# Attention scores of tiles 2 to 4 as three fp32r products of high and low parts instead of one fp32 product

## The chip, the cores and the metric

The kernel runs on one core of one Trainium2 chip. The metric is the device time of one execution in microseconds (us). Engines are named as the profile names them: PE (TensorE matmul), PEld (its weight loads), DVE (VectorE), ACT (ScalarE), POOL (GpSimd), SP (SyncE).

## The reference, cut to what matters

A block-causal attention over 8 batches of 8 heads (576 positions, head dimension 64, blocks of 64 positions), whose output goes into a mixture of experts with one expert per token.

```python
# q, k, v: (8, 8, 576, 64), all fp32
scores = scale * np.matmul(q, k.transpose(0, 1, 3, 2))      # scale = 1/8
mask = block_i >= block_j                                    # blocks of 64 positions
scores = np.where(mask, scores, -1000000000.0)
attn = np.exp(scores - np.max(scores, axis=-1, keepdims=True))
attn = attn / (np.sum(attn, axis=-1, keepdims=True) + 1e-09)
x = np.matmul(attn, v)                                       # -> (4608, 512)
...
# experts: 8 of them, 512 -> 1024 -> 512; the token's best expert by x @ w_gate
h = np.maximum(xe @ w1[e], 0.0)
out[mask] = gate_w[mask, None] * (h @ w2[e])
```

## The kernel before

The work has two parts in time: the attention, up to about 365 us of the profile, then the experts.

**Units, tiles, turns.** The attention goes through 32 units `m`; a unit is two heads of one batch, one in partitions 0 to 63 and one in 64 to 127 of the tiles `qd` and `kd` (queries and keys, head dimension in partitions). Its 576 query rows are a first block of 64 (tile 0) and four tiles of 128 (tiles 1 to 4). Tile `i` sees `e = 64 + 128 i` keys: 192, 320, 448 and 576. The products of tile `i` are one fp32 matmul per head (two for tile 4, whose 576 columns lie in two halves of 288): queries as weights, 64 rows by 128 columns, keys as the moving operand. PSUM names: tile 4's scores lie in `xa` and `xb` (first and second head), those of tiles 1 to 3 in `ya` and `yb`.

**The order of the work** is written out by hand in the table `ORDER`. One pass over it is a turn; a word such as `S4:2` means step `S4` for the unit `turn - 2`. In each turn every engine gets its instructions in the order of the table, and each engine works through its own strictly in that order. The steps that matter here:

- `ld` (SP): loads `qd`, `kd` and the values of a unit (three buffers each for the first two).
- `pQ` (POOL, L114): `q = 0.125 * qd`, 128x640, two buffers. It must wait for `S0` of the unit two before, the last to read that buffer.
- `S1` to `S4` (PE, L171): the scores. `S0` (PE, L160): those of tile 0, both heads in one matmul.
- `K`, `M` (DVE, L182, L187): mask of a block, row maximum. `E` (ACT, L202): exponential with row sums, written to `pb`.
- `R1`, `R2` (DVE): reciprocal of the sums. `Z` (POOL, L215): scales tile 0's row of probabilities, waits for `R2`.
- `T` (PE, L241): four 128x128 transposes of `pb` into one of two PSUM buffers `pt`. `H` (ACT, one of them on DVE; L253): copies it out to `ph`. `V` (PE, L272): probabilities times values, output `o`. `O`, `F`, `X`, `Y`: output copied, folded with the gate's weights, scaled.
- `y` (POOL): one item of a list, if there is one: a scatter of the router's table (an indirect DMA, L697), or one half of splitting a chunk of the first expert's weights (L1514, L1517). `z`: a piece of the router's work on DVE.

On PE a turn is: `Ta1, S0, S4, Tb1, Tk0, F1, Ta2, Tb2, F2, F0, Tx3, Tt0, S1, S2, S3, V0` to `V4`, `V5`; the next turn's `Ta1` follows. `E1` to `E3` of a unit fall at the end of the turn of its `S1` to `S3`, and the first transposes of the same unit open the next turn.

**fp32 and fp32r.** An fp32 matmul of the program shows as two instructions in the trace, an fp32r one as one. The experts' part already computes in fp32r: an operand `x` is split into a high part, `x` rounded to fp32r, and a low part, `x - high`, and a product is the sum of high*high, high*low and low*high in PSUM.

Of the kernel before, what the change touches and what calls it, by code (L numbers as in the profile page):

```python
# [8 lines left out]
F32 = mybir.dt.float32  # L9
F32R = mybir.dt.float32r  # L10
# [7 lines left out]
P = 128  # L18
H = 8
S = 576  # L20
D = 64
# [17 lines left out]
class Attention:  # L39
# [8 lines left out]
    def __init__(self, ctx, tc, ident, qT, kT, vt, w_gate, ends, po):  # L48
        self.tc, self.nc = tc, tc.nc
        self.qT, self.kT, self.vt = qT, kT, vt  # L50
        self.po = po

        self.ends = ends.rearrange("p (i c) -> p i c", c=P)
        self.M = qT.shape[0] * H // 2
        nc = self.nc
        cp = ctx.enter_context(tc.tile_pool(name="acst", bufs=1))
        self.raw = ctx.enter_context(tc.tile_pool(name="araw", bufs=3))
        self.rawv = ctx.enter_context(tc.tile_pool(name="arawv", bufs=5))
        self.spl = ctx.enter_context(tc.tile_pool(name="aspl", bufs=2))
        self.pt = ctx.enter_context(tc.tile_pool(name="apt", bufs=9))  # L60
        self.sm = ctx.enter_context(tc.tile_pool(name="asm", bufs=3))
        self.ot = ctx.enter_context(tc.tile_pool(name="aot", bufs=2))
        self.xp = ctx.enter_context(tc.tile_pool(name="axp", bufs=2))
        self.ps = ctx.enter_context(tc.tile_pool(name="psa", bufs=1, space=PSUM))
        self.ps_t = ctx.enter_context(tc.tile_pool(name="pst", bufs=2, space=PSUM))

        self.cp, self.ident = cp, ident
        self.raws, self.qs = {}, {}
        self.pb, self.sums, self.neg, self.rs = {}, {}, {}, {}
        self.bank, self.ptile, self.ph, self.oT, self.xs = {}, {}, {}, {}, {}  # L70
        self.small_bank, self.at = (None, None), {}
        self.used, self.later = {}, []
        self.op_ld(0)
        self.op_ld(1)
        self.zero = cp.tile([P, D], F32, tag="zero", name="zero")
        nc.vector.memset(self.zero, 0.0)

        self.h0 = [cp.tile([P, P], F32, tag=f"h0{i}", name=f"h0{i}") for i in range(2)]
        for t in self.h0:
            nc.gpsimd.memset(t, 0.0)  # L80
        self.p0 = {}
        self.o0 = [cp.tile([P, P], F32, tag=f"o0{i}", name=f"o0{i}") for i in range(2)]
        for t in self.o0:
            nc.gpsimd.memset(t, 0.0)
        self.eps = cp.tile([P, 9], F32, tag="eps", name="eps")
        nc.gpsimd.memset(self.eps, 1e-9)

        self.fold = cp.tile([P, H // 2, FC], F32, tag="fold", name="fold")
        nc.vector.memset(self.fold, 0.0)
        nc.scalar.copy(self.fold[:, :, 0:P], ident[:, None, :].to_broadcast([P, H // 2, P]))  # L90
        wg = w_gate.rearrange("(m j d) e -> j d m e", d=D, j=2)
        for j in range(2):
            nc.sync.dma_start(self.fold[D * j : D * j + D, :, P + E * j : P + E * j + E], wg[j])
# [17 lines left out]
    def op_pQ(self, m):  # L111

        q = self.qs[m] = self.spl.tile([P, 512 + P], F32, tag="q", name=f"q{m}")
        self.nc.gpsimd.tensor_scalar(q, self.raws[m][0][:, 0 : 512 + P], 0.125, None, ALU.mult)  # L114

    def banks(self, m, x):

        if (m, x) not in self.bank:
            shape, tag = ([P, 2, 512], "s" + x[1]) if x[0] in "xy" else ([P, 512], x[:2].rstrip("-"))
            self.bank[m, x] = (self.po if x == "o" else self.ps).tile(shape, F32, tag=tag, name=f"{x}{m}")  # L120
        return self.bank[m, x]
# [33 lines left out]
    def op_S(self, m, i):  # L155

        mm = self.nc.tensor.matmul
        q, k = self.qs[m], self.raws[m][1]
        if i == 0:
            mm(self.part(1, m, "S0", 432, 496), q[:, 512:], self.raws[m][0][:, 512 + P :], start=True, stop=True)  # L160
            return
        e = 64 + 128 * i
        for c in range(2 if i == 4 else 1):
            for j in range(2):
                out, _ = self.region(m, i, j)
                if i == 4:
                    out = out[:, c]
                n = out.shape[-1]
                o = (0 if j else S - e) + n * c
                r = slice(64 * j, 64 * j + 64)  # L170
                ins = mm(  # L171
                    out, q[r, 128 * (i - 1) : 128 * i], k[r, o : o + n], start=True, stop=True, skip_group_check=True
                )
                self.uses(m, i, j, ins)

    def op_K(self, m, i, j):

# [153 lines left out]
    def step(self, name, m):  # L331

        name, _, engine = name.partition("@")
        k = name[0]
        if name in ("ld", "pQ", "R1", "R2", "Z"):
            getattr(self, "op_" + name)(m)
        elif name in ("O", "O0"):
            getattr(self, "op_" + name)(m, engine)
        elif k == "H":
            self.op_H(m, name[1:], engine)  # L340
        elif k == "T":
            self.op_T(m, name[1:])
        elif k == "Y":
            self.op_Y(m, int(name[1]), engine)
        elif k in "KME":
            getattr(self, "op_" + k)(m, int(name[1]), int(name[2:] == "B"))
        else:
            getattr(self, "op_" + k)(m, int(name[1]))
# [65 lines left out]


ORDER = """
E3B:3 V5:4 z2:0 O0@D:4 ld:0 Ta1:3 O@A:4 Ha1@A:3 S0:3 S4:2 z6:0 M0:3 Tb1:3 Tk0:3 pQ:1 K4B:2 E0:3 R1:3 K4A:2 z1:0 M4B:2
R2:3 F1:4 Hb1@A:3 Ta2:3 Hk0@A:3 X1:4 Y1:4 M4A:2 Tb2:3 F2:4 E4B:2 y0:0 Z:3 Hb2@D:3 F0:4 Ha2@A:3 Y2:4 z4:0 Tx3:3 Tt0:3
E4A:2 X2:4 S1:2 z5:0 z0:0 z3:0 Ht0@A:3 Y0@D:4 S2:2 K1A:2 K2A:2 S3:2 K1B:2 Hx3@A:3 K2B:2 V0:3 V2:3 M2A:2 K3A:2 M1B:2
M3A:2 E2A:2 E1B:2 V1:3 y1:0 E3A:2 V3:3 M1A:2 K3B:2 M2B:2 E1A:2 M3B:2 V4:3 E2B:2  # L420
"""
# [397 lines left out]
class Experts:  # L819
# [62 lines left out]
    def run(self):  # L882
# [471 lines left out]
        def work(t):  # L1354

            engines = (dve, sp)
            to = ((lambda: blocks(t),), (lambda: move(sp, t),))
            plans = [[step(engine, i) if i > 1 else None for i in (t - 1, t)] for engine in engines]
            for engine, rest, (before, now) in zip(engines, to, plans):
                if t > 2:  # L1360
                    with engine.If(now[4] < 1):
                        for x in rest:
                            x()
                    engine.end_ifs()
                    units(engine, before, 1, split if engine is dve else refill(t - 1))
                units(engine, now, 0, split if engine is dve else refill(t))
                if t > 2:
                    with engine.If(now[4] > 0):
                        for x in rest:
                            x()  # L1370
                    engine.end_ifs()
# [229 lines left out]
```

## Time and profile before

| | |
|---|---|
| median of 3 runs | 809.85 us (809.34 to 810.65) |
| profiled execution | 810.1 us, its span 808.4 us |
| PE, ACT, DVE, POOL busy in the span | 781.2, 400.0, 471.8, 389.7 us |
| scores' matmuls (L171), columns 288: xa and xb, 128 instructions each | 41.6 us busy each |
| 320 and 448: ya and yb, 64 instructions each | 22.9 and 30.0 us busy each |
| pQ (L114), 32 times | 58.0 us busy, 1811 ns one |

A row of the timeline has start, duration, engine, line, operation, output and input by the program's names, the shape, the count, and in brackets the idle time of the engine before it with what ended it. [...] Rows of groups, with a bar, have busy time and mean duration of a group, then the idle time before it.

### The profile page before, as it was taken

What the parts mean: (1) busy time and instruction counts of PE and PEld (TensorE: products, weight loads), DVE (VectorE), ACT (ScalarE), POOL (GpSimd) and SP (SyncE); (2) the same over time, 40 slices, a digit from 0 to 9 for tenths busy, and PEclk for the clock granted to TensorE, in tenths of its full rate; (3) what the DMA queues carried; (4) which work ended last, traced back from release to release, by engine and by line L of the source; (5) the groups of instructions that cost most, each with busy time, mean ns of one, the idle gap of its engine ahead of it and who ended that gap; (6) DMA issues with size and microseconds to landing.
All of it is one profiled execution on the core that took longest, in us unless ns stands there. A gap on an engine that the chain in (4) does not pass through costs nothing.

```text
span 808.4 us, 17546 instructions
## 1 busy us (share of the span) xinstructions
PE 781.2 (97%) x4524; PEld 592.4 (73%) x4524; DVE 471.8 (58%) x1316; ACT 400.0 (49%) x1016; POOL 389.7 (48%) x397
## 2 busy tenths in 40 slices
PE   4999999999999999998999999999999999999995
PEld 2677666667776666766878888888888888888874
DVE  3566666776776777665855764412144713656963
ACT  3677777777777787772432323322332222323221
POOL 4122243344443362425456776555555555575663
PEclk9999999999999999999999999999999999999998
DMA  5234454646362626442337676744456564677762
GB/s 164 98 101 155 131 149 140 158 135 154 121 167 95 147 86 160 159 107 49 139 110 222 192 237 171 234 134 118 121 150 192 171 185 122 194 223 223 223 207 74
DMA packets 71120, 123.65 MB, mean 153 GB/s; under 512 B 16449, under 2 KB 37697, under 8 KB 70978
## 3 DMA queue, kind: packets, MB, share of 16 engines
q1 hardware_dynamic: 49858, 87.84, 37.4%
q0 software_dynamic: 7680, 20.50, 8.0%
q10 hardware_dynamic: 13440, 13.78, 6.3%
q8 instruction: 45, 0.74, 0.4%
q14 instruction: 97, 0.79, 0.4%
HBM read 73.09 MB, written 21.98 MB: 118 GB/s over the span
## 4 chain that ended last, share of the span: by engine, by line
PE 93%; POOL 2%; ACT 1%; issue 1%; DMA 1%; ACTq 1%; DVE 1%; DVEq 0%; POOLq 0%
PE py L1172 25%; PE o L272 12%; PE pt L1011 11%; PE ya L171 7%; PE o L1011 7%; PE ph L1011 7%; PE xa L171 5%; PE o L307 4%; PE o L301 1%; ACT pb L202 1%; PE o L160 1%; ACTq L1122 1%; DMA xg<-xd,idx 0%; POOL low L1145 0%; POOL tab L697 0%
## 5 line engine op out<-in xcount | busy, mean ns | idle before, releaser
L1172 PE MATMUL py<-w,low 128*128 (+1 forms) x912 | 217.3, 394 | 3.3 <-POOL low L1145 2.0
L1172 PEld LDWEIGHTS py<-w,low 128*128 128x128 f32 x912 | 172.0, 189 | 41.6 <-POOL low L1145 2.5
L114 POOL TENSOR_SCALAR q<-qd 128x640 f32<-128x640 f32 x32 | 58.0, 1811 | 186.7 <-PE o L160 133.4
L1190 ACT ACTIVATE y<-py,gates 128x512 f32<-128x512 f32 x35 | 24.1, 689 | 184.6 <-issue 129.5
L1145 POOL TENSOR_TENSOR low<-high,low 128x512 fp32r<-128x512 f32 x69 | 97.3, 1433 | 12.1 <-ACT low L1137 11.5
L980 POOL TENSOR_TENSOR xl<-high,xh 128x512 fp32r<-128x512 f32 x33 | 45.7, 1385 | 109.8 <-ACT xh L970 109.8
L1089 DVE STREAM_TRANSPOSE hblk<-xg 128x512 f32<-128x512 f32 x35 | 24.8, 709 | 87.9 <-DMA xg<-xd,idx 84.6
L202 ACT ACTIVATE pb<-ya,neg 128x320 f32<-128x320 f32 (+2 forms) x96 | 50.1, 525 | 48.1 <-DVE neg L187 48.1
L1011 PE MATMUL pt<-w,xh 128*128 x272 | 70.8, 392 | 0.0
L1333 DVE TENSOR_TENSOR w<-raw,w 128x1024 f32 x48 | 68.0, 1456 | 0.0
L1330 DVE CAST w<-raw 128x1024 f32 x48 | 56.8, 1222 | 16.0 <-issue 12.6
L171 PE MATMUL ya<-kd,q 64*128 64x192 f32 (+2 forms) x192 | 61.8, 456 | 2.7 <-ACT pb L202 2.7
L171 PE MATMUL yb<-kd,q 64*128 64x192 f32 (+2 forms) x192 | 61.8, 456 | 0.0
L1011 PEld LDWEIGHTS pt<-w,xh 128*128 128x128 f32 x272 | 51.0, 188 | 11.1
L697 POOL DMA_INDIRECT tab<-toks,posi x40 | 41.5, 1037 | 28.8 <-DVE run L664 14.8
L918 POOL DMA_INDIRECT xg<-xd,idx x39 | 44.0, 1128 | 19.3 <-POOL idx L910 17.2
L202 ACT ACTIVATE pb<-yb,neg 128x192 f32<-128x192 f32 (+2 forms) x96 | 49.8, 526 | 0.2 <-DVE neg L187 0.2
L1137 ACT CAST low<-high 128x1024 fp32r<-128x1024 f32 x35 | 36.6, 1045 | 26.5 <-DMA high<-hblk 26.5
L1101 DVE STREAM_TRANSPOSE hblk<-pt 128x512 f32<-128x512 f32 x34 | 23.4, 705 | 43.4 <-ACT pt L1048 43.4
L171 PE MATMUL xa<-kd,q 64*128 64x288 f32 x128 | 41.6, 447 | 6.6 <-POOL q L114 6.6
L307 PE MATMUL o<-fold,oT 128*128 128x144 f32 x256 | 43.9, 294 | 1.1 <-ACT oT L279 0.6
L187 DVE TENSOR_REDUCE neg<-yb 128x1 f32<-128x192 f32 (+2 forms) x96 | 42.8, 474 | 3.3
(1013 smaller groups left out, 1775.1 us busy)
## 6 DMA issues: line engine op xcount, KB each, us to landing
raw<-w SPq DMA_DIRECT2D x52, 512.0 KB, 4.9
high<-hblk SPq DMA_DIRECT2D x280, 48.0 KB
high<-hblk ACTq DMA_DIRECT2D x280, 48.0 KB
qd<-qT SPq DMA_DIRECT2D x32, 352.0 KB, 3.1
v<-vt SPq DMA_DIRECT2D x32, 352.0 KB, 4.8
kd<-kT SPq DMA_DIRECT2D x32, 288.0 KB, 3.8
xd<-xt SPq DMA_DIRECT2D x7, 1026.0 KB, 8.9
xd<-xg SPq DMA_DIRECT2D x9, 256.5 KB, 7.0
```

The costliest lines, as they stand in the source:

```text
L114: self.nc.gpsimd.tensor_scalar(q, self.raws[m][0][:, 0 : 512 + P], 0.125, None, ALU.mult)
L171: ins = mm(out, q[r, 128 * (i - 1) : 128 * i], k[r, o : o + n], start=True, stop=True, skip_group_check=True)
L202: ins = self.nc.scalar.activation(dst, src, AF.Exp, bias=self.neg[m][:, c : c + 1], scale=1.0, accum_out=self.sums[m][:, c : c + 1])
L272: self.nc.tensor.matmul(out[r], self.raws[m][2][:, slot], self.ph[m, bank][:, c0:c1], start=t in (0, 5), stop=t in (4, 5), skip_group_chec ...
L307: mm(t[:, i], self.oT[m, 0][:, o : o + P], w, start=True, stop=True)
L918: pool.indirect_dma_start(out=self.xg[i], out_offset=None, in_=self.xd[:, :], in_offset=bass.IndirectOffsetOnAxis(ap=self.idx[:, t : t + 1 ...
L980: pool.tensor_sub(xl, r, xh).then_inc(sem["xp"], 1)
L1011: m = pe.matmul(ph[f], x[:, P * k : P * k + P], weights(k, f, part), start=start and k == 0, stop=stop and k == 3,)
L1145: engine.tensor_sub(hl[:, c], h[:, c], hh[:, c]).then_inc(sem["ln" if engine is pool else "le"], 1)
L1172: m = pe.matmul(self.py[t % 2], h[:, c // 4, P * (c % 4) : P * (c % 4) + P], wf[:, bass.ds(off + (base + 512 * c), 512)], start=n == 0, st ...
L1330: dve.tensor_copy(part(c, 0), raw[c % 4]).then_inc(sem["wh"], 1)
L1333: dve.tensor_sub(part(c, 1), raw[c % 4], part(c, 0)).then_inc(sem["wd"], 1)
```

## The change

For the units from 2 on, `S2`, `S3` and `S4` become three fp32r products each. The parts come from four new steps:

- `gK` (ACT): `kh`, the keys rounded to fp32r, 128x576. `lK` (POOL): `kl = kd - kh`.
- `gQ` (POOL): `qh`, the scaled queries of tiles 2 to 4 rounded to fp32r, 128x384, by adding a zero. `lQ` (POOL): `ql = q - qh`.

Tile 1 and tile 0 stay in fp32. In the table, `pQ` moves from behind `Tk0` to behind `Z`, with a third `y` step ahead of it; `lK`, `gQ` and `lQ` follow it, and `gK` stands between `E0` and `R1`.

```diff
+    def high_low(self, m, k, n):
+        pool = self.hk if k == "k" else self.hq           # two buffers each
+        self.hilo[m, k] = [pool.tile([P, n], F32R, tag=k + x, name=f"{k}{x}{m}") for x in "hl"]
+        return self.hilo[m, k][0]
+    def op_gQ(self, m):
+        if m > 1:
+            hi = self.high_low(m, "q", 384).rearrange("p (a b) -> p a b", b=D)
+            x = self.qs[m][:, P:512].rearrange("p (a b) -> p a b", b=D)
+            self.nc.gpsimd.tensor_add(hi, x, self.zero[:, None, :].to_broadcast([P, 6, D]))
+    def op_lQ(self, m):
+        if m > 1:
+            hi, lo = self.hilo[m, "q"]
+            self.nc.gpsimd.tensor_sub(lo, self.qs[m][:, P:512], hi)
+    def op_gK(self, m):
+        if m > 1:
+            self.nc.scalar.copy(self.high_low(m, "k", S), self.raws[m][1])
+    def op_lK(self, m):
+        if m > 1:
+            hi, lo = self.hilo[m, "k"]
+            self.nc.gpsimd.tensor_sub(lo, self.raws[m][1], hi)
...
     def op_S(self, m, i):
...
+        at = P * (i - 1)
+        terms = ((q, k),)
+        if m > 1 and i > 1:
+            (qh, ql), (kh, kl) = self.hilo[m, "q"], self.hilo[m, "k"]
+            terms, at = ((qh, kh), (qh, kl), (ql, kh)), at - P
         for c in range(2 if i == 4 else 1):
+            for a, (q, k) in enumerate(terms):
                 for j in range(2):
...
-                    out, q[r, 128 * (i - 1) : 128 * i], k[r, o : o + n], start=True, stop=True, skip_group_check=True
+                    out, q[r, at : at + P], k[r, o : o + n], start=a == 0, stop=a == len(terms) - 1,
...
-... M0:3 Tb1:3 Tk0:3 pQ:1 K4B:2 E0:3 R1:3 K4A:2 ...
+... M0:3 Tb1:3 Tk0:3 K4B:2 E0:3 gK:1 R1:3 K4A:2 ...
-... y0:0 Z:3 Hb2@D:3 F0:4 ...
+... y0:0 Z:3 y2:0 pQ:1 lK:1 gQ:1 lQ:1 Hb2@D:3 F0:4 ...
```

Three places in the order of instructions, around the turn whose `Ta1` is that of unit 17. Numbers behind a tile's letters are the unit; those behind the underscore only tell tiles apart.

PE, tiles 1 to 3 of unit 18 (`ya18`, `yb18`), before:

```order
L238 MATMUL pt17t0_2772<-ident_68,p017_2585 64x128
L171 MATMUL ya18_2776<-kd18_2398,q18_2575 128x192
L171 MATMUL yb18_2778<-kd18_2398,q18_2575 128x192
L171 MATMUL ya18_2776<-kd18_2398,q18_2575 128x320
L171 MATMUL yb18_2778<-kd18_2398,q18_2575 128x320
L171 MATMUL ya18_2776<-kd18_2398,q18_2575 128x448
L171 MATMUL yb18_2778<-kd18_2398,q18_2575 128x448
```

and in the change:

```order
L207 MATMUL ya18_3209<-kd18_2762,q18_3016 128x192
L207 MATMUL yb18_3211<-kd18_2762,q18_3016 128x192
L207 MATMUL ya18_3209<-kh18_2974,qh18_3019 128x320
L207 MATMUL yb18_3211<-kh18_2974,qh18_3019 128x320
L207 MATMUL ya18_3209<-kl18_2975,qh18_3019 128x320
L207 MATMUL yb18_3211<-kl18_2975,qh18_3019 128x320
L207 MATMUL ya18_3209<-kh18_2974,ql18_3020 128x320
L207 MATMUL yb18_3211<-kh18_2974,ql18_3020 128x320
L207 MATMUL ya18_3209<-kh18_2974,qh18_3019 128x448
L207 MATMUL yb18_3211<-kh18_2974,qh18_3019 128x448
```

The 192 columns of tile 1 still come from `kd` and `q`; tile 2's pair has become three pairs into the same PSUM region, and tile 3's the same. Tile 4, at the start of the turn, has six pairs of 288 columns.

ACT around `Hb1` (the copy `ph17b1`), before:

```order
L279 COPY oT16_2692<-o16_2646 128x512
L253 COPY ph17a1_2694<-pt17a1_2687 128x512
L202 ACTIVATE p017_2585,sums17_2581<-o2116_2674,neg17_2582 128x64
L253 COPY ph17b1_2732<-pt17b1_2705 128x512
L253 COPY ph17k0_2739<-pt17k0_2710 128x512
```

and in the change:

```order
L316 COPY oT16_3108<-o16_3062 128x512
L290 COPY ph17a1_3110<-pt17a1_3103 128x512
L239 ACTIVATE p017_2983,sums17_2979<-o2116_3090,neg17_2980 128x64
L139 CAST kh19_3141<-kd19_2932 128x576
L290 COPY ph17b1_3157<-pt17b1_3129 128x512
L290 COPY ph17k0_3164<-pt17k0_3134 128x512
```

The cast of unit 19's keys stands ahead of `Hb1`.

POOL, from one `q` to the next, before (`p016` is what `Z` scales):

```order
L114 TENSOR_SCALAR q18_2575<-qd18_2397 128x640
L697 DMA tab_58<-toks_146,posi2_2421 43008x1
L215 TENSOR_SCALAR p016_2445<-p016_2445,rs16_2443 128x64
L697 DMA tab_58<-toks_146,posi2_2421 43008x1
L570 MEMSET L3_2677 64x8
```

and in the change:

```order
L734 DMA tab_58<-toks_156,posi2_2793 43008x1 x2
L252 TENSOR_SCALAR p016_2818<-p016_2818,rs16_2816 128x64
L734 DMA tab_58<-toks_156,posi2_2793 43008x1
L117 TENSOR_SCALAR q18_3016<-qd18_2761 128x640
L144 TENSOR_TENSOR kl18_2975<-kd18_2762,kh18_2974 128x576
L130 TENSOR_TENSOR qh18_3019<-q18_3016,zero_139 128x384
L135 TENSOR_TENSOR ql18_3020<-q18_3016,qh18_3019 128x384
```

`q18` now comes behind `Z` of unit 16 and the third scatter of the turn, and three splits follow it.

More of the change, by code (lines that the diff above doesn't have):

```diff
@@ L59, in __init__ @@
         self.spl = ctx.enter_context(tc.tile_pool(name="aspl", bufs=2))
+        self.hk = ctx.enter_context(tc.tile_pool(name="ahk", bufs=2))
+        ctx.enter_context(tc.tile_pool(name="apart", bufs=1)).tile([P, 16], F32, tag="apart", name="apart")
+        self.hq = ctx.enter_context(tc.tile_pool(name="ahq", bufs=2))
         self.pt = ctx.enter_context(tc.tile_pool(name="apt", bufs=9))
@@ L67, in __init__ @@
         self.cp, self.ident = cp, ident
-        self.raws, self.qs = {}, {}
+        self.raws, self.qs, self.hilo = {}, {}, {}
         self.pb, self.sums, self.neg, self.rs = {}, {}, {}, {}
@@ L162, in op_S @@
         e = 64 + 128 * i
-        for c in range(2 if i == 4 else 1):
[L164 to L171, printed above, removed]
-                    out, q[r, 128 * (i - 1) : 128 * i], k[r, o : o + n], start=True, stop=True, skip_group_check=True
-                )
-                self.uses(m, i, j, ins)
+        at = P * (i - 1)
[3 more added lines that the diff above has]
+            terms, at = ((qh, kh), (qh, kl), (ql, kh)), at - P
+        for c in range(2 if i == 4 else 1):
+            for a, (q, k) in enumerate(terms):
+                for j in range(2):
+                    out, _ = self.region(m, i, j)
+                    if i == 4:
+                        out = out[:, c]
+                    n = out.shape[-1]
+                    o = (0 if j else S - e) + n * c
+                    r = slice(64 * j, 64 * j + 64)
+                    ins = mm(
+                        out, q[r, at : at + P], k[r, o : o + n], start=a == 0, stop=a == len(terms) - 1,
+                        skip_group_check=True,
+                    )
+                    self.uses(m, i, j, ins)
     def op_K(self, m, i, j):
@@ L334, in step @@
         k = name[0]
-        if name in ("ld", "pQ", "R1", "R2", "Z"):
+        if name in ("ld", "pQ", "gQ", "lQ", "gK", "lK", "R1", "R2", "Z"):
             getattr(self, "op_" + name)(m)
@@ L416 @@
 ORDER = """
-E3B:3 V5:4 z2:0 O0@D:4 ld:0 Ta1:3 O@A:4 Ha1@A:3 S0:3 S4:2 z6:0 M0:3 Tb1:3 Tk0:3 pQ:1 K4B:2 E0:3 R1:3 K4A:2 z1:0 M4B:2
-R2:3 F1:4 Hb1@A:3 Ta2:3 Hk0@A:3 X1:4 Y1:4 M4A:2 Tb2:3 F2:4 E4B:2 y0:0 Z:3 Hb2@D:3 F0:4 Ha2@A:3 Y2:4 z4:0 Tx3:3 Tt0:3
+E3B:3 V5:4 z2:0 O0@D:4 ld:0 Ta1:3 O@A:4 Ha1@A:3 S0:3 S4:2 z6:0 M0:3 Tb1:3 Tk0:3 K4B:2 E0:3 gK:1 R1:3 K4A:2 z1:0 M4B:2
+R2:3 F1:4 Hb1@A:3 Ta2:3 Hk0@A:3 X1:4 Y1:4 M4A:2 Tb2:3 F2:4 E4B:2 y0:0 Z:3 y2:0 pQ:1 lK:1 gQ:1 lQ:1 Hb2@D:3 F0:4 Ha2@A:3 Y2:4 z4:0 Tx3:3 Tt0:3
 E4A:2 X2:4 S1:2 z5:0 z0:0 z3:0 Ht0@A:3 Y0@D:4 S2:2 K1A:2 K2A:2 S3:2 K1B:2 Hx3@A:3 K2B:2 V0:3 V2:3 M2A:2 K3A:2 M1B:2
```

## The prediction

> **What bounds the kernel now.** I read the page's totals, the windows, then PE's timeline over one turn. First, from the page, busy times, two rows of the 40 slices, and the chain that ended last:
>
> ```profile
> span 808.4 us, 17546 instructions
> ...
> PE 781.2 (97%) x4524; PEld 592.4 (73%) x4524; DVE 471.8 (58%) x1316; ACT 400.0 (49%) x1016; POOL 389.7 (48%) x397
> ...
> PEclk9999999999999999999999999999999999999998
> ...
> PE 93%; POOL 2%; ACT 1%; issue 1%; DMA 1%; ACTq 1%; DVE 1%; DVEq 0%; POOLq 0%
> ```
>
> The profiled execution lasted 810.1 us around this span of 808.4; the median of the three runs is 809.85. The chain is PE nearly throughout, at full clock. Windows, one over most of the attention part and one over a single turn:
>
> ```profile
> core 0: us, PE busy (x) PEld busy (x) DVE busy (x) ACT busy (x) POOL busy (x), PEclk, DMA share, GB/s
> 49.00:340.00 291.00, 290.90 (x2216) 201.98 (x2214) 202.95 (x823) 223.29 (x678) 112.12 (x107) 1.00 0.50 139
> 203.90:214.69 10.79, 10.79 (x86) 7.47 (x82) 8.15 (x32) 8.40 (x27) 4.32 (x4) 1.00 0.30 97
> ```
>
> A turn lasts 10.79 us, all of it PE; ACT works 8.40 and POOL 4.32 of that. What PE saves here is worth its full amount, up to the point where another engine takes over. PE's timeline of that turn (start, duration, shape; durations overlap, so I use distances between starts):
>
> ```profile
> 203.90 0.66 PE L241 MATMUL pt17a<-ident,pb 128*128 128x128 f32 x4
> ...
> 204.66 0.51 PE L171 MATMUL xa<-kd,q 64*128 64x288 f32 x1
> 204.66 0.51 PE L171 MATMUL xb<-kd,q 64*128 64x288 f32 x1
> 205.00 0.40 PE L171 MATMUL xa<-kd,q 64*128 64x288 f32 x1
> ...
> 205.25 0.40 PE L171 MATMUL xa<-kd,q 64*128 64x288 f32 x1
> ...
> 205.49 0.40 PE L171 MATMUL xa<-kd,q 64*128 64x288 f32 x1
> ...
> 205.83 0.66 PE L241 MATMUL pt17b<-ident,pb 128*128 128x128 f32 x4
> ...
> 210.02 0.43 PE L171 MATMUL ya<-kd,q 64*128 64x320 f32 x1
> ...
> 210.29 0.43 PE L171 MATMUL ya<-kd,q 64*128 64x320 f32 x1
> ...
> 210.56 0.54 PE L171 MATMUL ya<-kd,q 64*128 64x448 f32 x1
> ...
> 210.94 0.54 PE L171 MATMUL ya<-kd,q 64*128 64x448 f32 x1
> ...
> 211.41 1.08 PE L272 MATMUL o<-ph17k,v 128*64 128x512 f32 x4
> ...
> 214.69 0.66 PE L241 MATMUL pt18a<-ident,pb 128*128 128x128 f32 x4
> ```
>
> Each fp32 matmul of the program is two instructions here, and the two heads (xa, xb; 64 rows each) run side by side: both start at 204.66. One instruction takes 0.2425 us for 288 columns (205.00 to 205.49 is two), 0.27 for 320, 0.375 for 448, that is 0.84 ns a column.
>
> **The change, part by part.**
>
> *Scores on PE.* Removed per unit: tile 4 has two halves of two instructions, tiles 2 and 3 two each: 4 x 0.2425 + 2 x 0.27 + 2 x 0.375 = 2.26 us. Added: three fp32r products for each, so 6 steps of 288, 3 of 320 and 3 of 448 columns, again both heads side by side. No fp32r matmul of 64 rows is in the trace; the nearest are those of 128 rows and 512 columns. From the chain, the piece where transposes give way to fp32r:
>
> ```profile
> 390.97 0.55 PE pt L1056 x5
> 391.51 5.51 PE py L1172 x24
> ```
>
> 24 matmuls in 5.51 us: 229.6 ns each, 0.448 ns a column. At half the fp32 instruction's 0.84 the 512 columns would take 215. So a step costs N x 0.42 ns (121, 134 and 188 ns) and something on top. If what is on top (229.6 - 215 = 15 ns) belongs to each matmul, the steps take 136, 149 and 203 ns and the unit 1.87 us; if it goes by columns (0.448), 129, 143 and 201, and 1.81. I take a value between, 133, 147 and 202: 1.85 us, and **0.41 us saved a unit**. Bounds: with nothing on top it is 1.69, saving 0.57; with both heads' products paying their 15 ns one after the other, 30 a step, it is 2.05, saving 0.21. The chain also shows transposes in fp32 followed by fp32r without a gap (390.97 + 0.55 is 391.52), so I cost the switch between tile 1 (still fp32) and tile 2 at nothing; its other end is in the rivals.
>
> *Weight loads.* Every product loads its own 128 columns. Loads at the start of tile 4, where nothing covers the first pair:
>
> ```profile
> 204.66 0.18 PEld L171 LDWEIGHTS xa<-kd,q 64*128 64x128 f32 x1
> 204.66 0.18 PEld L171 LDWEIGHTS xb<-kd,q 64*128 64x128 f32 x1
> 204.76 0.19 PEld L171 LDWEIGHTS xa<-kd,q 64*128 64x128 f32 x1
> 204.77 0.19 PEld L171 LDWEIGHTS xb<-kd,q 64*128 64x128 f32 x1
> 205.01 0.19 PEld L171 LDWEIGHTS xa<-kd,q 64*128 64x128 f32 x1
> ```
>
> The second load of each head begins 0.10 to 0.11 us after the first, for both heads at once: a load occupies its half for about 0.105 us, and the halves load in parallel. It then lies under the running matmul: xa's load at 205.01 falls inside xa's matmul of 205.00, and the next matmul follows 0.25 later with no gap. The shortest new step, 0.121 to 0.136 us, still covers 0.105, so loads cost nothing; the margin is only 16 to 31 ns. If the cover is gone, 0.105 us is added 12 times a unit.
>
> [...]
>
> *ACT: the keys' high part (gK), 128x576, between E0 and Hb1.* Casts of two sizes, and ACT around the place:
>
> ```profile
> L970 ACT CAST xh<-high 128x512 fp32r<-128x512 f32 x33 | 20.1, 610 | 5.1 <-issue 5.1
> L1137 ACT CAST low<-high 128x1024 fp32r<-128x1024 f32 x35 | 36.6, 1045 | 26.5 <-DMA high<-hblk 26.5
> ...
> 211.87 0.53 ACT L202 ACTIVATE pb<-ya,neg 128x320 f32<-128x320 f32 x1 [1.44 <-DVE neg L187]
> ...
> 216.12 0.24 ACT L202 ACTIVATION_READ_ACCUMULATOR p<-o,neg 128x1 f32 x1
> 217.31 0.59 ACT L253 COPY ph18b<-pt18b 128x512 f32<-128x512 f32 x1 [0.95 <-PE pt18b L241]
> ```
>
> 0.85 ns for each further column: 576 take 0.66 us, on ACT some 0.55 since neighbours overlap. It fills the 0.95 us in which ACT waited for Tb1. That gap narrows: ACT's row from 211.87 on hangs on tile 2, and PE gains behind that tile 0.14 (tile 3) and 0.17 (tile 4), so 0.64 is left for 0.55. Cost nothing, margin 0.1. Were PE to gain the full 0.57 a unit, the gap would be 0.52 (0.19 and 0.24 less) and ACT would cap the gain near 0.55. Behind gK waits Hb1, for it Ta2 and with it PE; each 0.1 us that gK overruns costs up to 3 us in 30 turns.
>
> *POOL: pQ is moved behind Z and a third y step (y2); lK, gQ, lQ are new.* Splits of 512 columns, and this turn's rows that set the start:
>
> ```profile
> L1514 POOL TENSOR_TENSOR high<-xg,zero 128x512 fp32r<-128x512 f32 x8 | 10.2, 1273 | 0.0
> L1517 POOL TENSOR_TENSOR low<-xg,high 128x512 fp32r<-128x512 f32 x8 | 10.2, 1271 | 0.2
> ...
> 206.87 1.02 POOL L697 DMA_INDIRECT tab<-toks,posi  x1 [0.17 <-issue]
> ...
> 206.99 0.20 DVE L211 RECIPROCAL rs<-rs 128x9 f32<-128x9 f32 x1
> ...
> 215.62 1.81 POOL L114 TENSOR_SCALAR q<-qd 128x640 f32<-128x640 f32 x1 [6.02 <-PE o L160]
> 218.66 0.44 POOL L215 TENSOR_SCALAR p<-p,rs 128x64 f32<-128x64 f32 x1
> ```
>
> By columns: lK 1.43, gQ and lQ 0.96 each, 3.35 us more a turn, 7.7 to 8.1 in all. Z waits for the reciprocal, which ends 3.3 us into the turn. Then Z 0.44, a y2 with its issue 1.2, pQ 1.81, lK 1.43, gQ 0.96 (until 9.1) and lQ (until 10.1). PE wants the queries' high part when S4 of the next turn starts, 0.76 us (204.66 - 203.90) behind a turn of 10.38: at 11.1, and the low part two steps later. So PE waits for nothing here, with 2.0 and 1.3 us in hand; a scatter that holds POOL longer than that would be paid by PE in full. The y steps only come earlier: scatters and weight splits are the same in number, and a third step a turn fits (9.3 us with three). kd is read a turn earlier, by gK instead of S4; it was loaded in the turn before that.
>
> **Sum.** 30 units (2 to 31) x 0.41 = 12.3 us; from 810.1 to 797.8. Against the median, which lies 0.25 lower, **797.5 us**. The experts' part only starts earlier.
>
> **The rivals.**
>
> *ACT or POOL takes over* (or the switch to fp32r empties PE once a turn, 0.1 us for the gap at 205.73 to 205.83 where PE changes from 64 rows to 128, and 0.1 for a bare load). Half of the saving goes: 0.2 x 30 = 6 us, 804. For it: ACT's margin of 0.1. Against it: ACT 8.95 of 10.38, POOL 8.1 of 10.38.
>
> *The loads come into the open.* Each step is then 0.105 longer than bare streaming: 0.226, 0.239 and 0.293, the unit 2.95 us against 2.26, 0.69 lost, 20.8 us; 830. This ends on the other side. It decides from (2.26 - 1.69)/12 = 47 ns over bare streaming a step: above, the kernel is slower. Were loads only taken in turn by the two halves, a step could not be under 0.21, the unit 2.52 to 2.6, and the time 818 to 820. For it: nothing in the trace streams 288 columns in 121 ns over a load. Against it: the rows of 204.66 to 205.01.
>
> [...]
>
> *No change* (within 0.2%, 1.6 us, about what a measurement of this kernel can tell): overhead near 47 ns a step.
>
> **How the numbers follow.** Forecast (793 to 803): 0.70. A half gain (803 to 808): 0.14. No change: 0.03. Slower: 0.13, of it loads 0.09, halves 0.04. So faster 0.84, same 0.03, slower 0.13. The range runs from the capped 0.55 a unit (16.5 us, 793) past the half gain to 807, and leaves out what is slower.
>
> **What would show it.** Right: a turn of about 10.4 us; 288-column steps of one head 0.13 to 0.14 us apart; loads under them; Hb1 without a long wait; ACT's cast ending before Tb1 does; PE not waiting for POOL ahead of S4; MoE rows unchanged. Wrong: steps of 0.21 or more; PE idle ahead of S4 released by POOL's ql; PE idle ahead of Ta2 released by ACT.

## The result, and the profile after

The changed kernel takes 816.02 us (median of 7 runs, 815.49 to 821.64) against 810.65 (809.34 to 811.89, 7 runs) for the kernel before on the same chip: a ratio of 1.0085, interval 1.0068 to 1.0101. It is slower by 0.9%, where the prediction had it 1.5% faster. The profiled execution has a span of 813.8 us.

Lines of the kernel after are 36 or 37 higher than before: the scores' L171 is L207, the maxima's L187 is L224, the masks' L182 is L219, the exponentials' L202 is L239. pQ's L114 is L117; new are L139 (gK), L144 (lK), L130 (gQ) and L135 (lQ). First the page: totals, then the chain that ended last by engine.

```profile
span 813.8 us, 18256 instructions
...
PE 777.4 (96%) x4764; PEld 606.3 (75%) x4764; DVE 487.2 (60%) x1316; ACT 415.6 (51%) x1046; POOL 489.5 (60%) x487
...
PE 70%; DVE 7%; issue 7%; ACT 4%; DMA 3%; SPq 3%; ACTq 2%; POOL 1%; DVEq 1%; POOLq 0%
```

PE is busy 3.8 us less than before and yet the span is 5.4 us longer, and the chain is PE for 70% instead of 93%. DVE has the same 1316 instructions as before, but 15.4 us more busy time. The window over most of the attention part says the same (columns: the stretch, then its length, and busy time and count of PE, PEld, DVE, ACT and POOL, PE's granted clock, DMA share, GB/s):

```profile
49.00:340.00 291.00, 281.86 (x2382) 209.41 (x2379) 219.49 (x807) 232.49 (x693) 194.94 (x182) 1.00 0.50 139
```

PE was busy 290.90 of 291 us here; now 9 us are idle. DVE does fewer instructions (807 for 823, since the work is behind by then) in 16.5 us more.

**Where PE works as forecast.** A turn without router work, from the timeline of the changed kernel (start, duration, engine and line, shape):

```profile
61.63 0.66 PE L278 MATMUL pt4a<-ident,pb 128*128 128x128 f32 x4
62.39 0.40 PE L207 MATMUL xa<-kh,qh 64*128 64x288 f32 x1
62.63 0.29 PE L207 MATMUL xa<-kl,qh 64*128 64x288 f32 x1
62.63 0.19 PEld L207 LDWEIGHTS xa<-kh,ql 64*128 64x128 f32 x1
62.76 0.29 PE L207 MATMUL xa<-kh,ql 64*128 64x288 f32 x1
...
63.16 0.29 PE L207 MATMUL xa<-kh,ql 64*128 64x288 f32 x1
...
63.31 0.71 ACT L139 CAST kh<-kd 128x576 fp32r<-128x576 f32 x1
63.38 0.66 PE L278 MATMUL pt4b<-ident,pb 128*128 128x128 f32 x4
...
64.07 0.58 ACT L290 COPY ph4b<-pt4b 128x512 f32<-128x512 f32 x1
...
72.00 0.66 PE L278 MATMUL pt5a<-ident,pb 128*128 128x128 f32 x4
```

From `Ta1` to the next `Ta1` it is 10.37 us; the forecast was 10.38. The steps of 288 columns are (63.16 - 62.63) / 4 = 0.13 us apart, and the weights of the next step are loaded under the running one (the PEld row). From tile 4's first product to `Tb1` it is 0.99 us, where it was 1.17.

**Where the time went.** The groups of DVE in the window 49 to 340, before and then after; four small instructions (mean ns of one stands behind the busy time):

```profile
L599 DVE SCALAR_TENSOR_TENSOR at<-w,base 128x5 f32<-128x5 f32 x6 | 0.9, 155 | 0.0
L692 DVE SCALAR_TENSOR_TENSOR posi<-r,at 128x5 int32<-128x5 int32 x6 | 0.9, 155 | 0.0
L666 DVE TENSOR_TENSOR run<-run,oh 64x8 bf16<-64x8 bf16 x6 | 0.9, 153 | 0.2
L208 DVE TENSOR_TENSOR rs<-sums,eps 128x9 f32<-128x9 f32 x27 | 4.0, 149 | 0.0
```

```profile
L636 DVE SCALAR_TENSOR_TENSOR at<-w,base 128x5 f32<-128x5 f32 x6 | 6.1, 1012 | 0.0
L729 DVE SCALAR_TENSOR_TENSOR posi<-r,at 128x5 int32<-128x5 int32 x6 | 4.4, 727 | 0.0
L703 DVE TENSOR_TENSOR run<-run,oh 64x8 bf16<-64x8 bf16 x6 | 3.8, 631 | 0.2
L245 DVE TENSOR_TENSOR rs<-sums,eps 128x9 f32<-128x9 f32 x26 | 6.2, 239 | 0.0
```

An instruction on 5 elements a partition goes from 155 ns to 1012. The timeline of a turn with router work shows during what (changed kernel, DVE, POOL, ACT and the next `Ta1`):

```profile
231.90 1.42 POOL L144 TENSOR_TENSOR kl<-kd,kh 128x576 fp32r<-128x576 f32 x1
...
232.05 0.20 DVE L696 TENSOR_REDUCE more<-oh 128x8 f32<-128x32 bf16 x1
...
232.16 1.18 DVE L729 SCALAR_TENSOR_TENSOR posi<-r,at 128x5 int32<-128x5 int32 x1
...
233.28 1.01 POOL L130 TENSOR_TENSOR qh<-q,zero 128x384 fp32r<-128x384 f32 x1
233.45 0.86 DVE L703 TENSOR_TENSOR run<-run,oh 64x8 bf16<-64x8 bf16 x1
...
234.53 0.30 DVE L219 MEMSET ya<- 64x64 f32 x2
...
235.54 0.53 ACT L239 ACTIVATE pb<-ya,neg 128x320 f32<-128x320 f32 x1 [2.71 <-DVE neg L224]
...
237.68 0.66 PE L278 MATMUL pt20a<-ident,pb 128*128 128x128 f32 x4 [0.78 <-issue]
```

`posi` ends at 233.34, with `kl` (233.32); `run` at 234.31, with `qh` (234.29). Each began under the POOL instruction and ended with it. Both read two operands from SBUF. `more`, a reduction of one SBUF operand, ran under the same `kl` in 0.20 us, its time in the kernel before. Behind them in DVE's order stand the masks and maxima of tiles 1 to 3 (`ya`): the mask begins at 234.53. ACT's first exponential waits for the maximum for 2.71 us instead of 1.44, and the first transposes of the next turn, which read those exponentials, find PE idle for 0.78 us. That is the path: POOL's split, DVE's small instruction, DVE's queue, ACT, PE.

### The profile page after: what moved, and what is told of

Its sections match the earlier page's. It is cut to its first block, busy times and chain, and to the rows that moved or that the text cites. A ratio compares the mean times of both kernels' runs of the same rounds, so it can differ in the third digit from the quotient of the medians.

```text
span 813.8 us, 18256 instructions
## 1 busy us (share of the span) xinstructions
PE 777.4 (96%) x4764; PEld 606.3 (75%) x4764; DVE 487.2 (60%) x1316; ACT 415.6 (51%) x1046; POOL 489.5 (60%) x487
## 4 chain that ended last, share of the span: by engine, by line
PE 70%; DVE 7%; issue 7%; ACT 4%; DMA 3%; SPq 3%; ACTq 2%; POOL 1%; DVEq 1%; POOLq 0%
PE py L1209 17%; PE o L309 9%; PE pt L1048 8%; PE ph L1048 5%; PE ya L207 5%; PE o L1048 5%; PE xa L207 3%; PE o L344 3%; ACT pb L239 3%; ACTq L1159 2%; SPq L1159 2%; PE xb L207 1%; DMA xg<-xd,idx 1%; DVE neg L224 1%; PE o L190 1%
## 5 line engine op out<-in xcount | busy, mean ns | idle before, releaser
L1017 POOL TENSOR_TENSOR xl<-high,xh 128x512 fp32r<-128x512 f32 x33 | 47.7, 1445 | 106.4 <-ACT xh L1007 106.3
L1182 POOL TENSOR_TENSOR low<-high,low 128x512 fp32r<-128x512 f32 x69 | 95.6, 1407 | 13.3 <-ACT low L1174 10.9
L252 POOL TENSOR_SCALAR p<-p,rs 128x64 f32<-128x64 f32 x32 | 14.2, 444 | 122.6 <-DVE rs L248 54.2
L239 ACT ACTIVATE pb<-ya,neg 128x320 f32<-128x320 f32 (+2 forms) x96 | 50.0, 524 | 60.2 <-DVE neg L224 58.6
L1370 DVE TENSOR_TENSOR w<-raw,w 128x1024 f32 x48 | 64.8, 1389 | 0.0
L1367 DVE CAST w<-raw 128x1024 f32 x48 | 53.3, 1151 | 15.0 <-issue 13.2
L117 POOL TENSOR_SCALAR q<-qd 128x640 f32<-128x640 f32 x32 | 58.1, 1816 | 1.1 <-DMA qd<-qT 0.8
L734 POOL DMA_INDIRECT tab<-toks,posi x40 | 41.0, 1024 | 19.0 <-issue 15.4
L239 ACT ACTIVATE pb<-yb,neg 128x192 f32<-128x192 f32 (+2 forms) x96 | 49.7, 526 | 0.2 <-DVE neg L224 0.2
L1231 POOL DMA_INDIRECT out<-y,idx x35 | 36.8, 1053 | 15.6 <-ACT y L1227 10.6
L224 DVE TENSOR_REDUCE neg<-yb 128x1 f32<-128x192 f32 (+2 forms) x96 | 42.8, 474 | 3.3
L144 POOL TENSOR_TENSOR kl<-kd,kh 128x576 fp32r<-128x576 f32 x30 | 42.5, 1416 | 0.0
```

What stands on the lines that cost most here:

```text
L224: ins = self.nc.vector.tensor_reduce(self.neg[m][:, c : c + 1], src, AX.XY if i == 4 else AX.X, ALU.max, negate=True)
L239: ins = self.nc.scalar.activation(dst, src, AF.Exp, bias=self.neg[m][:, c : c + 1], scale=1.0, accum_out=self.sums[m][:, c : c + 1])
L1017: pool.tensor_sub(xl, r, xh).then_inc(sem["xp"], 1)
L1182: engine.tensor_sub(hl[:, c], h[:, c], hh[:, c]).then_inc(sem["ln" if engine is pool else "le"], 1)
L1367: dve.tensor_copy(part(c, 0), raw[c % 4]).then_inc(sem["wh"], 1)
L1370: dve.tensor_sub(part(c, 1), raw[c % 4], part(c, 0)).then_inc(sem["wd"], 1)
```

## The experiments

**Theory A:** a split on POOL that reads two operands from SBUF holds DVE's instructions that read or write SBUF, until the POOL instruction ends. **B:** POOL is too slow, and PE or ACT waits for its results. **C:** the fp32r products themselves, or PE's signals among them, cost the time. A useful number beside the times is the distance of `S0` of unit 1 from that of unit 31 (30 turns, in the trace the starts of `o<-qd,q`): 325.9 us before, 331.3 in the change, 313.6 by the forecast. The ratio of a run is to the kernel before, measured beside it.

### The router's steps ahead of the splits

`e1_router_early`: four of the router's DVE steps stand behind `M0`, early in the turn, instead of late, under the splits.

```diff
-... M0:3 Tb1:3 ... Y2:4 z4:0 Tx3:3 Tt0:3 ... S1:2 z5:0 z0:0 z3:0 Ht0@A:3 ...
+... M0:3 z4:0 z5:0 z0:0 z3:0 Tb1:3 ... Y2:4 Tx3:3 Tt0:3 ... S1:2 Ht0@A:3 ...
```

> The changed kernel with four of the router's DVE steps (z4, z5, z0, z3) moved from the middle of the turn, where POOL makes the parts, to behind M0, where POOL does not. Theory A (a POOL split with two inputs holds DVE's instructions between SBUF tiles until it ends, and DVE's order carries the hold to E2, E1 and the next Ta1): the turns of 11.6 to 11.8 us go to 10.4 to 10.6, the time to 799 to 804. Theory B (POOL is late with the parts, PE waits for ql ahead of S4): nothing moves, 814 to 818. Theory C (PE's completion signals come late while a scatter and the loads are issued): only the turns around 10.9 are concerned, 813 to 817.

Measured: 802.12 us (801.01 to 802.82), ratio 0.9893 (0.9864 to 0.9923); 30 turns 318.2 us. POOL's work is the same and the time is 14 us lower than the change's. This version beats both kernels. Its groups of DVE in the same window:

```profile
L636 DVE SCALAR_TENSOR_TENSOR at<-w,base 128x5 f32<-128x5 f32 x7 | 1.5, 216 | 0.0
L703 DVE TENSOR_TENSOR run<-run,oh 64x8 bf16<-64x8 bf16 x6 | 1.0, 167 | 0.2
```

From 1012 and 631 ns back to 216 and 167.

### Splits only once

`e2_fixed_parts`: the parts are made for unit 2 alone and read by all later units, so all fp32r products stay and POOL's splits go.

```diff
     def op_gQ(self, m):
-        if m > 1:
+        if m == 2:
...
+        elif m > 2:
+            self.hilo[m, "q"] = self.hilo[2, "q"]
```

(and likewise for the keys.)

> The changed kernel without the splits: all units from 3 on multiply the high and low parts of unit 2 (so the scores, and with them the routing and the experts' part, are other ones; only the attention's turns are compared). A and B: every turn is 10.3 to 10.5 us, the attention part ends some 11 to 12 us earlier than before the change. If fp32r products themselves cost what was lost (in turns with the router's work), turns of 11 us and more stay.

Measured: 800.31 us (one run); 30 turns 313.0 us, 0.6 from the forecast. The same window:

```profile
49.00:340.00 291.00, 290.90 (x2536) 220.95 (x2534) 212.89 (x858) 231.49 (x704) 114.62 (x111) 1.00 0.53 143
```

PE is busy 290.90 of 291 us again, as before the change, and has done more (2536 instructions; a unit takes 10.36 us). The fp32r products and their loads give 325.9 - 313.0 = 12.8 us in 30 units, 0.43 a unit. C falls for the products. The moved `pQ` and the third `y` step are in this run too, so the new order alone costs nothing.

### Splits that nobody reads

`e3_splits_unused`: the parts are made and the products stay in fp32.

```diff
-        if m > 1 and i > 1:
+        if False:
             (qh, ql), (kh, kl) = self.hilo[m, "q"], self.hilo[m, "k"]
```

> The splits are made as in the change, but all scores stay single fp32 products. A: router turns are held up as in the change, 11.2 to 11.9 us against 10.79, the time 815 to 828. B: PE waits for no part, so 809 to 812. C: 809 to 813.

Measured: 821.54 us (820.37 to 822.04), ratio 1.0129 (1.01 to 1.0158); 30 turns 337.6 us. Nobody waits for the parts here, so B falls: the splits cost 337.6 - 325.9 = 11.7 us by being there. ACT's cast and the new order are in this run as well, but its first four turns, which have them too and no router step under the splits, last 10.79 us as before. One row of its groups:

```profile
L636 DVE SCALAR_TENSOR_TENSOR at<-w,base 128x5 f32<-128x5 f32 x6 | 5.6, 934 | 0.0
```

### Splits that read one operand

`e4_one_input`: the same three POOL instructions with a number as second operand.

```diff
-            self.nc.gpsimd.tensor_add(hi, x, self.zero[:, None, :].to_broadcast([P, 6, D]))
+            self.nc.gpsimd.tensor_scalar(hi, x, 1.0, None, ALU.mult)
...
-            self.nc.gpsimd.tensor_sub(lo, self.raws[m][1], hi)
+            self.nc.gpsimd.tensor_scalar(lo, self.raws[m][1], 0.0001, None, ALU.mult)
```

> The changed kernel with POOL's three part instructions replaced by ones of the same shapes with a single input (high part: times 1, low parts: times 0.0001, so the low parts are not the real ones). A, if the hold needs two inputs on POOL: DVE's small instructions are back at 0.15 to 0.2 us, the time 798 to 806. A, if any POOL instruction holds DVE: 813 to 820. B: follows POOL's own time; a single-input instruction of 640 columns takes 1.81 us, so the three take 1.2 to 1.6 each, and 814 to 820.

Measured: 799.01 us (798.47 to 800.13), ratio 0.9858 (0.983 to 0.9887); 30 turns 315.0 us, 16.3 less than the change, in the change's own order of work. POOL's instructions got longer, not shorter (`kl` 1.65 us for 1.42, the queries' 1.17 for 1.00), and DVE is held far less:

```profile
266.57 1.65 POOL L144 TENSOR_SCALAR kl<-kd 128x576 fp32r<-128x576 f32 x1
266.58 0.68 DVE L701 TENSOR_TENSOR run<-run,more 128x8 bf16<-128x8 bf16 x1
```

`run<-run,more` begins under `kl` and ends 0.96 us ahead of it; in the change such a step ends with it. So what holds DVE to the end is the kind of POOL instruction, not how long it lasts. The operation changes along with the operands here (TENSOR_TENSOR becomes TENSOR_SCALAR), and no run separates the two.

With e1 and e3 this shows A, but A as worded is too wide. In the attention parts of all fourteen traces (before, the change, the twelve runs), of the DVE instructions that began under a two-operand POOL instruction with at least 0.35 us of it left, 119 of 120 that read two operands from SBUF were held to its end, and so were all 40 of two small ones with one operand (TENSOR_SCALAR `g<-g`, COPY `xt<-g`). Of the reductions and reciprocals with one operand in SBUF, 81 of 82 ended before it.

### One operand where the values stay the same

`e5_high_one_input`: e1's order; the high parts of queries and of the expert's weights by a multiplication with 1.0.

```diff
-            self.nc.gpsimd.tensor_add(hi, x, self.zero[:, None, :].to_broadcast([P, 6, D]))
+            self.nc.gpsimd.tensor_scalar(hi, x, 1.0, None, ALU.mult)
...
-                nc.gpsimd.tensor_add(split(hi), split(w), z)
+                nc.gpsimd.tensor_scalar(hi, w, 1.0, None, ALU.mult)
```

> e1_router_early's order, and the high parts of queries and weights are made on POOL by a multiplication with 1.0 that reads one operand from SBUF, instead of an addition of a zero that reads two; the low parts (two operands) stay. The values are the same. In e1_router_early five turns are still long (11.15 to 11.91 us against 10.36), and in each a router's step on DVE ends together with a two-input POOL instruction. If the hold goes with the two reads, about half of these steps (those over the high parts: at, posi under gQ; g and L,m under the weights' high part) shrink from up to 1.1 us to 0.3 to 0.75, and the time falls from 802.1 to about 799.5 (798 to 801). If long turns come from the amount of router work on DVE or from POOL's own length, nothing changes: 801.5 to 803.

Measured: 806.53 us (806.18 to 807.47), ratio 0.9937 (0.9918 to 0.9957): a miss; 30 turns 322.6 us, 4.4 more than e1. The holds under the high parts did shrink (`L<-L,m` under a weights' part: 0.49 us, where it was 1.14 in e1). But turns that were 10.36 us in e1 are now 11.0 to 11.25. One of them, DVE and ACT behind tile 4's last product:

```profile
147.78 0.98 POOL L734 DMA_INDIRECT tab<-toks,posi  x1 [0.30 <-issue]
147.81 0.29 PE L207 MATMUL xb<-kh,ql 64*128 64x288 f32 x1
...
148.04 0.66 PE L278 MATMUL pt12b<-ident,pb 128*128 128x128 f32 x4
...
149.37 0.58 ACT L290 COPY ph12b<-pt12b 128x512 f32<-128x512 f32 x1 [0.71 <-PE pt12k L278]
149.43 0.11 DVE L219 MEMSET xb<- 64x64 f32 x1 [2.05 <-PE pt12k L278]
```

`xb`'s last product ends at 148.10, yet the mask that waits for it begins at 149.43, and ACT's copy of `pt12b` (whose transposes end at 148.70) at 149.37: 1.33 and 0.67 us behind PE, while PE's instructions go on. Where nothing is late, the mask begins 0.16 us behind (e9's rows below). DVE has nothing ahead in its queue there. The change has the same in 8 of its turns, beside two scatters close behind each other, one on either side of tile 4's products.

### The scatter moved by 0.2 and by 0.6 us

`e9_scatter_later` is e1 and `e10_scatter_past` is e5, each with a MEMSET on POOL ahead of `y0`, of 128x320 in e9 and 128x640 in e10:

```diff
                 if name[0] == "y":
+                    if name == "y0":
+                        self.nc.gpsimd.memset(self.pad, 0.0)
                     other()
```

> e1_router_early with one addition: a MEMSET of 128x320 on POOL (about 0.35 us by the sizes of the page) ahead of y0 in every turn, with nobody waiting for it. In the turns with two scatters it moves the start of the second one from 0.84 to 0.93 us behind the turn's S0 (e1_router_early) to about 1.1 to 1.2, which is where it stands in two turns of the change and in six of e5_high_one_input, in each of which PE's completion signals of S4 and of the transposes behind it arrive 0.5 to 1.2 us late. If the late signal comes from where the scatter's issue falls against S4, the six turns 8, 12, 16, 20, 24 and 28 get it here too and last about 11.05 us instead of 10.36: 806 (805 to 808). If it does not depend on that place, or comes from the one-input multiplications, the time stays at 802 (801 to 803.5).

> e5_high_one_input with the same addition, 128x640 (about 0.6 us): the second scatter moves from 1.00 to 1.32 us behind S0 to 1.5 to 1.8, past the end of S4 (1.33). If the place of the scatter's issue makes the signal late, the six to eight turns of 11.0 to 11.25 us fall to 10.4 to 10.5, and the time from 806.5 to 802 or below (800 to 803), below e1_router_early if the one-input multiplications are worth something. If not, 806 to 807.

Measured: e9 803.93 us (802.1 to 804.64), ratio 0.9927 (0.9901 to 0.9954), 30 turns 317.7 us; e10 804.7 us (804.2 to 805.0), ratio 0.9942 (0.9919 to 0.9965), 30 turns 318.4 us. Both times lie just outside the ranges that were expected, so their turns decide. In e10 the six two-scatter turns are 10.36 us, so the late signals go when the scatters are pulled apart, and 30 turns are 4.1 us shorter than in e5. But in e9 the second scatter begins 1.10 to 1.21 us behind `S0`, at e5's place, and no signal is late:

```profile
149.08 0.29 PE L208 MATMUL xb<-kh,ql 64*128 64x288 f32 x1
...
149.16 0.97 POOL L737 DMA_INDIRECT tab<-toks,posi  x1 [0.17 <-issue]
...
149.53 0.11 DVE L220 MEMSET xb<- 64x64 f32 x1 [0.88 <-PE xb L208]
```

So the place of the second scatter alone does not make them late. Nor do the places of both: in the change, the turn that `S0` of unit 25 opens has its scatters 0.42 us ahead of `S0` and 0.92 us behind it, and the mask comes 1.21 us behind `xb`'s last product; in e1, the turn of unit 24 has them at 0.41 and 0.93 us, and the mask comes 0.16 us behind. What makes the signals late stays open; e2 (products without splits) and e3 (splits without products) show none of them.

### Two items a turn, and the change once more

`e8_two_items`: the change without its last list item of a turn (`y1:0` taken from the table). `e7_change_again`: the change, one more profile.

> The change without its last y step (y1): two items of POOL's list a turn instead of three, none at the end of a turn, so no scatter is issued beside S4 of the next turn and no weights' split runs past the turn's end. In the change 8 turns have a late completion signal of PE at S4 (0.5 to 1.1 us) beside such a scatter. If the scatter beside S4 makes the signal late, no turn here has one, and the time falls by 8 x 0.5 to 1.0 us: 809 to 813. If the hold by the query and key splits is nearly all, the time is 814 to 817, with router turns as long as in the change (up to 11.8 us).

> The changed kernel as it is, one more profile. If the 8 late signals at S4 belong to the program, they are in the same turns (those starting at 119, 151, 162, 195, 206, 250, 296 and 341 us) and turn lengths agree with the first profile within 0.05 us; if they belong to that one execution, they are elsewhere or gone, and the long turns without them stay (10.9 to 11.5 us by the hold alone). Time 815.5 to 818.

e7: 815.74 us (one run), with the late signals in the same 8 turns, whose lengths agree within 0.15 us (turn 9: 11.28 and 11.40; 0.05 was expected, and the other turns agree within 0.21). They belong to the program. e8: 834.56 us (833.84 to 837.07), ratio 1.029 (1.0262 to 1.0318), far outside what was expected: 30 turns 344.8 us. Five turns carry a hold that no other run shows, one of them from its timeline:

```profile
122.25 1.85 POOL L117 TENSOR_SCALAR q<-qd 128x640 f32<-128x640 f32 x1
...
123.33 3.14 DVE L630 TENSOR_TENSOR oh<-cd,w 128x40 bf16<-128x40 f32 x1
...
124.04 1.42 POOL L144 TENSOR_TENSOR kl<-kd,kh 128x576 fp32r<-128x576 f32 x1
...
125.40 1.01 POOL L130 TENSOR_TENSOR qh<-q,zero 128x384 fp32r<-128x384 f32 x1
...
126.48 1.00 POOL L135 TENSOR_TENSOR ql<-q,qh 128x384 fp32r<-128x384 f32 x1
```

One DVE instruction on 40 elements, 0.20 us when nothing holds it, lasts 3.14 us and ends at 126.47: through the rest of `pQ`, all of `kl` and all of `qh`, which follow each other without a gap. It gets through only in the gap ahead of `ql`. Why it got through at neither earlier place is open: in the change the same instruction, begun 1.03 us into `pQ`, took 0.20 us there, and `posi` got through between `kl` and `qh`.

### Where else the router's steps could stand

`e6_early_and_one_input` is e5 with the two steps that open a turn moved behind `M0`; `e11_router_behind_R2` and `e12_router_behind_M4A` are e1 with its four steps behind `R2` and behind `M4A`.

```diff
e6   -E3B:3 V5:4 z2:0 O0@D:4 ... S4:2 z6:0 M0:3 z4:0 ...
     +E3B:3 V5:4 O0@D:4 ... S4:2 M0:3 z2:0 z6:0 z4:0 ...
e11  -... M0:3 z4:0 z5:0 z0:0 z3:0 Tb1:3 ... R2:3 F1:4 ...
     +... M0:3 Tb1:3 ... R2:3 z4:0 z5:0 z0:0 z3:0 F1:4 ...
e12  +... M4A:2 z4:0 z5:0 z0:0 z3:0 Tb2:3 ...
```

> e5_high_one_input, and the two router steps that open a turn (z2, and z6 behind it) stand behind M0 of the same turn, where the last weights' split of the turn before is over; so no router step stands in the first 1.3 us of a turn, nor in its last half. By the theory of the hold the long turns left are those in which a scatter or a load is late, and no router turn is longer than about 10.8 us: 797.5 (796.5 to 799.5), as the prediction had it for the whole change. If router work on DVE costs PE time wherever it stands, 800 to 802 as in e5 or worse, since the block of steps behind M0 gets longer and delays K4B.

> e1_router_early, but the four router steps (z4, z5, z0, z3) stand behind R2 instead of behind M0, so behind K4B and K4A, the first steps of tile 4's maximum; in e1_router_early the turns 9, 13 and 17 (11.6 to 11.9 us) have K4B waiting 1.3 us behind them in DVE's own order. POOL's splits begin 4.9 us into the turn, the steps stand at about 3 to 4.5. If DVE's order is what makes these turns long, they fall to about 10.6 to 10.9 and the time to 799 (797.5 to 800.5). If the steps only delay another step of DVE or ACT there (X1, Y1, M4A, Hb1), 801 to 804; if they slip under the splits, more.

> The same four steps behind M4A, one place further: behind all of tile 4's maxima, at about 4 to 5.5 us of the turn, at the edge of the splits (kl from 4.9 us). By DVE's order alone nothing of attention is late that PE needs: 798 (796.5 to 800). By the hold the last of the four steps falls under kl (1.42 us) in the turns with router work, 7 or 14 times up to 1.3 us on Hb2 and E4B behind it: 801 to 808.

All three miss. e6: 809.43 us (807.65 to 811.24), ratio 0.9968 (0.9954 to 0.9981); the longer block ahead of `K4B` makes that mask 1.0 us late in four more turns, beside the late signals of e5. e11: 803.89 us (803.6 to 804.55), ratio 0.9935 (0.9912 to 0.9958); `K4B` is on time, but the router's own matmul, which stands in PE's order behind these steps, waits for one of them 7 times, 5.6 us in all. e12: 831.72 us (829.95 to 832.07), ratio 1.0269 (1.0243 to 1.0295), and not by the hold, which is 1.2 us at most there:

```profile
99.65 0.15 DVE L703 TENSOR_TENSOR run<-run,oh 64x8 bf16<-64x8 bf16 x1
99.80 1.19 POOL L734 DMA_INDIRECT tab<-toks,posi  x1 [7.82 <-DVE run L703]
101.04 0.46 POOL L252 TENSOR_SCALAR p<-p,rs 128x64 f32<-128x64 f32 x1
...
101.55 0.30 PE L275 MATMUL pt7t<-ident,p 128*64 128x128 f32 x1 [1.43 <-POOL p L252]
```

The step that a scatter waits for now comes after the scatter's place in POOL's order. POOL waits 7.82 us, `Z` behind it is late, and PE idles 1.43 us for `Z`.

## Why the prediction was wrong, point by point

**PE's saving, 0.41 us a unit: right.** Steps of 288 columns are 0.13 us apart (forecast 0.133). A unit saves 0.42 us in a turn without router work (10.79 to 10.37) and 0.43 over all turns of e2.

**Loads hidden: right.** No step shows 0.105 us on top: the steps of 288 columns are 0.13 us apart with a load under each, so the second rival (830 us, 0.226 us a step) falls. `xa` and `xb` take these steps at the same time (both `kh,ql` products start at 62.76), so the 0.04 given to the halves, the two heads not running side by side, falls as well.

**gK in ACT's gap, margin 0.1: right.** The cast is 0.71 us (forecast 0.66), ends at 64.02, and `Hb1` begins at 64.07, as pt4b's transposes end. PE idle ahead of `Ta2` released by ACT, one of the signs of being wrong, does show in turns with late signals, but there ACT had ended the cast and was itself waiting for PE, as in the rows of e5.

**POOL's timetable: right.** `kl` is 1.42 us (forecast 1.43), `qh` and `ql` 1.00 each (0.96), and PE waits for none of them.

**"So PE waits for nothing here", for the splits on POOL: the step that failed.** It asked only whether POOL is done in time, and not what a POOL instruction takes from another engine while it runs; so the sum has no term for the splits, where e3 measured 11.7 us. The mechanism of the first rival (an engine takes over, 804) was another one: neither ACT nor POOL had too much work of its own. What POOL took shows in the trace of the change: a DVE instruction of 155 ns (`at<-w,base`) lasts up to 1.40 us there and ends with POOL's two-operand one. Under e4's one-operand `kl` such an instruction was not held to the end: `run<-run,more` was through 0.96 us ahead of it. The attention part of the kernel before has no such case to read it from: 24 DVE instructions began there under a two-operand POOL instruction with at least 0.35 us of it left, and none of them reads two operands from SBUF. That DVE's small steps lay in the splits' slot could be read ahead of time from the order of the work; before the change POOL was idle there.

**The sum.** Over 30 turns, in us: the products give -12.8 (e2), the splits +11.7 (e3). The change is at +5.5 (331.3 - 325.9), so 6.6 remain. The 8 turns with late signals last 89.4 us in the change and 82.9 in e2, 6.5 more, but e3, which has no late signal, already loses 2.0 in three of these turns; so 4.4 of the 6.6 falls to them. The rest lies in the other 22 turns, which lose 11.8 against e2 where they lose 9.7 in e3: the hold seems to cost more in the shorter turns, which no run tests. So the hold alone (11.8 and 2.0) took back what the products gained (12.8), and 4.4 of the 5.5 us of loss fall to the turns with late signals. The first cause is shown by e1, e3 and e4; of the second it is shown where it strikes, not why. The experts' part did not change: from the last `S0` to the end of the span it is 451.5 us before (808.4 - 356.9) and 451.4 after (813.8 - 362.4).

## What to carry to other kernels

When work goes to POOL, look not only at whether POOL has time: list what DVE runs in the same microseconds. Two-operand work on POOL belongs beside DVE instructions that read PSUM or reduce one SBUF tensor (here the maxima of 448 columns kept their 615 ns and `more` its 0.20 us) and not beside DVE's small steps with two SBUF operands (`at<-w,base` went from 155 to 1012 ns), whose queue feeds everybody else. Moving four small steps took 14 us off here (e1; no run moved the splits), but each engine's order has to be followed: every step moved has a waiter on POOL, ACT or PE with a place of its own.

## What the runs showed of the hardware that was not expected

- A two-operand POOL instruction (128x384 to 128x576, 1.0 to 1.4 us) held DVE instructions with two operands in SBUF to its end (119 of 120), small SBUF copies and tensor-scalars too (40 of 40). Reductions and reciprocals of one SBUF operand ran on beside it (81 of 82), and so did DVE instructions with a source in PSUM: a maximum of 448 columns (`neg`) takes 615 ns before and in the change. In e8 one of 0.20 us was held 3.14 us, through several POOL instructions without a gap.
- A one-operand POOL instruction of 1.5 to 1.9 us (`pQ` 1.8, e4's `kl` 1.65, e5's weights' part 1.49) held DVE instructions with two SBUF operands mostly at its start: those that began in its first 0.6 us ended 0.6 to 0.8 us after its start, and most that began later took their usual 0.15 to 0.20 us. (The instruction of e8 is an exception, and `g<-g` and `xt<-g` were in part held to the end.) It was slower itself: 1.17 us instead of 1.00 for 128x384 (e4, e5), 1.49 instead of 1.28 for 128x512 (e5).
- fp32r products of two heads, 64 rows each, ran side by side at 0.13, 0.145 and 0.20 us a step for 288, 320 and 448 columns, with a weight load each under them.
- PE's completion signal reached DVE and ACT 0.5 to 1.2 us late while PE worked on, in the same eight turns of both profiled executions of the change. In e10, whose second scatter stands 0.25 to 0.75 us later than in e5, it is gone; but the same places of both scatters gave a late signal in the change and none in e1. Its cause is open.
